# Seven sums of weights for the odd column tiles are formed in chunk 0 and not in chunk 1

## The chip, the cores and the metric

The kernel runs on one core of a Trainium2 chip, in fp32. The metric is the device time of one execution in microseconds; the time of a kernel is the median of its runs.

## What is computed

The reference runs a gated linear recurrence per batch and head, and a SwiGLU block on its output:

```
q, k, v, f_logit: (4, 8, 768, 48)
f = sigmoid(f_logit)
for t in range(768):
    state = f[t, :, None] * state + outer(k[t], v[t])
    y[t] = q[t] @ state
x = y as (4*768, 8*48) = (3072, 384)
out = (silu(x @ w_gate) * (x @ w_val)) @ w_out        # w_gate, w_val: (384, 1536), w_out: (1536, 384)
```

The weights come as float64 and are turned into fp32 on the chip.

## The kernel before

The 768 positions are cut into six chunks of 128. A chunk holds the 128 positions of all four batches, 512 tokens. Attention of a chunk is run batch by batch in steps (`attention`): gates through a sigmoid on ScalarE and, from chunk 2 on, a transpose on VectorE (L510, L511; the loads arrive in tiles called squares); a scan of the gates (L519), small steps (L522 to L524), kT (L531, L537), a second scan (L539) and qT (L532, L540) on VectorE; scores `sc` and transposed keys `kt` on TensorE (L552, L559), the masked scores `A` on VectorE (L554); the outputs `y` and the state's increment `dS` on TensorE (L578, L582, L606), and the state on VectorE (L610, L544). The steps of chunk c+1 are dealt out among the pieces of the feed-forward block of chunk c by `take_turns`, evenly by the number of pieces.

Chunk 0's feed-forward block is plain (`mlp_plain`). For 12 column tiles of 128 it runs gate and val products (L666), a silu on ScalarE (L678) and a product on VectorE (L682); then the down products (L690), which end in copies to `ob` (L695). Between these pieces stand calls of `weights`, each of which fetches a piece of weights by a transfer from SyncE's queue, splits an earlier one on ScalarE (L447, L449) and joins a still earlier one on VectorE in four instructions (L455 to L459). The joined gate and val weights stand together in `w_both`.

Chunks 1 to 5 use a scheme with 15 products for a 3 x 3 by 3 x 2 block product (`mlp_fifteen`) and one with seven for the down products (`down_seven`). The 15 products are run for each of four column tiles j, in the order 0, 2, 1, 3; the text calls the 15 products of one j a triple, as they come in three pieces. They need sums of blocks of the weights. Six of the results go to a tile of their own, `extra` (e0 to e5), formed by seven sums; nine sums are written into `w_both` itself, so they can only be formed after the plain products of chunk 0. Each sum is one VectorE instruction over 128 x 512 elements (`plus` L728, `minus` L731). `weight_sums(odd)` returns the 16 sums for the even (0) or the odd (1) column tiles. The even ones are needed from the first triple of chunk 1 on, the odd ones from the third.

In a triple the products of one name add up in one PSUM bank: A has two banks, B one, and the names o and c share two. After most products ScalarE copies the running sum out, to `c11` and so on or to `aside` (L841), and VectorE adds or subtracts it (L728, L731). Finished parts go through silu (L852) and a product on VectorE (L853) into `h`. A product into a bank waits for the copy of what stood there. The sigmoid and the silu need different tables on ScalarE, so a table load stands at each change between them.

What sets the order: the framework emits each engine's instructions into an in-order queue. A scheduler may move an instruction past others when it builds the queues; `keep_order` ties chosen instructions of an engine together. `chained` does so for the products and the copies of the triples. `behind(f)` ties what f emits to the last VectorE instruction emitted before it. `weave(first, second)` deals out the functions of `second`, two at a time, as pieces of their own among those of `first`, each pair through `behind`.

The lists of pieces are put together at the end of `short_path`, in the loop over the chunks. In chunk 0, `hidden` holds 24 gate and val pieces and 12 calls of `weights`, a call after every second piece, and `last` the 16 steps of the down products with four more calls. Before the change the 16 even sums are woven into `last`, and the 16 odd ones into the first half of chunk 1's pieces, so that

```
pieces = hidden + weave(last, weight_sums(0))
hidden = hidden[:1] + weave(hidden[1:half], weight_sums(1)) + hidden[half:]
```

Of the kernel before, what the change touches and what calls it, by code (L numbers as in the profile page):

```python
# [289 lines left out]
def short_path(ctx, tc, ident, least, judge, q, k, v, f_logit, moe_w_gate, moe_w_val, moe_w_out, out):  # L290
# [105 lines left out]
    def make_rooms(pool):  # L396
        for nm in "fkq":
            rooms[nm] = pool.tile([128, Q + HP * RUN], FP32, tag=f"{nm}squares", name=f"{nm}squares")
            nc.gpsimd.memset(rooms[nm][:, HP * RUN:], 0.0)
# [11 lines left out]
    def load(u):  # L411
        b, c = units[u]
        rows = slice(c * C, (c + 1) * C)
        for nm, src in (("f", f_logit), ("k", k), ("q", q)):
            if c >= SQUARES:
                for n in range(4):
                    at = Q * (1 - n % 2)
                    nc.sync.dma_start(
                        out=rooms[nm][Q * n:Q * (n + 1), at:at + HP * RUN].rearrange("t (a e) -> t a e", a=HP),
                        in_=src[b, n // 2::2, rows, :].rearrange("a (t i) d -> t a (i d)", i=NI))  # L420
                continue
            nc.sync.dma_start(out=raw[nm][u % NRAW][:, :, 0:D], in_=src[b, :, rows, :].rearrange("h t d -> t h d"))
        nc.sync.dma_start(out=v_of(u)[:, :, 0:D], in_=v[b, :, rows, :].rearrange("h t d -> t h d"))
# [205 lines left out]
    def attention_steps(c):  # L629

        runs = [attention(c * B + b) for b in range(B)]
        parts = [1, 2, 1, 2]
        order = sorted((2 * b + s, b, n) for b in range(B) for s, n in enumerate(parts))
        return [lambda b=b, n=n: [next(runs[b]) for _ in range(n)] for _, b, n in order]
# [11 lines left out]
    def keep_order(mine):  # L646
        for a, b in zip(mine, mine[1:]):
            tc.add_manual_dep(b, a.name, mybir.DependencyInfo(mybir.DependencyClass.NoSync,
                                                              mybir.DependencyReason.DATA), reason="order")
# [10 lines left out]
    def mlp_plain(c):  # L660
        h = {}

        def product(w, j, name):
            p = fps.tile([128, 512], FP32, tag="m", name=name)[:, 0:TB]
            for i in range(KT):
                nc.tensor.matmul(p, lhsT=w[:, i, j * 128:(j + 1) * 128], rhs=xT[c][:, i, :],  # L666
                                 start=(i == 0), stop=(i == KT - 1))
            return p

        def part(j):  # L670
            if j % NP not in h:
                h[j % NP] = hidden_tile()
            k = 2 * (j // NP)
            return h[j % NP][:, k:k + 2, :].rearrange("p a t -> p (a t)")

        def gate(j):
            p = product(w_gate, j, "gate")
            nc.scalar.activation(part(j), p, AF.Silu)  # L678

        def val(j):  # L680
            p = product(w_val, j, "val")
            nc.vector.tensor_tensor(part(j), part(j), p, ALU.mult)  # L682

        return ([lambda j=j, f=f: f(j) for i in range(0, NF, 2) for f in (gate, val) for j in (i, i + 1)],
                downs_abreast(c, h))
# [52 lines left out]
    def every_second(t, odd):  # L738

        return t.rearrange("p g (n two r) -> p g n two r", two=2, r=128)[:, :, :, odd, :]  # L740

    def weight_parts():
        w = {(i, k): w_both[:, :, k, i * NG:(i + 1) * NG] for i in range(KT) for k in range(KT)}
        e = [extra[:, n] for n in range(6)]
        return w, e

    def weight_sums(odd):

        w, e = weight_parts()
        w = {n: every_second(t, odd) for n, t in w.items()}  # L750
        e = [every_second(t, odd) for t in e]
        a11, a12, a13, a21, a22, a23, a31, a32, a33 = (w[i, k] for i in range(3) for k in range(3))
        return [lambda f=f, d=d, x=x, y=y: f(d, x, y) for f, d, x, y in (
            (minus, e[0], a11, a12), (plus, e[1], a12, a33), (plus, e[1], e[1], a13), (minus, e[2], e[1], a11),
            (minus, e[3], e[0], a13), (plus, e[4], a21, a32), (minus, e[5], a12, a21),
            (minus, a11, a12, a23), (plus, a13, e[3], a21), (plus, e[3], e[3], a23), (plus, a13, a13, a31),
            (minus, a13, a13, a33), (minus, a21, a22, a21), (plus, a22, a22, a23), (plus, a22, a22, a32),
            (minus, a31, a32, a31))]
# [237 lines left out]
    def weave(first, second):  # L996

        second = [second[i:i + 2] for i in range(0, len(second), 2)]
        woven = []
        for i, f in enumerate(first):  # L1000
            woven += [f] + [lambda fs=fs: behind(lambda: [g() for g in fs]) for fs in
                            second[i * len(second) // len(first):(i + 1) * len(second) // len(first)]]
        return woven

    def behind(f):

        n = len(traced)
        last = next(ins for ins in reversed(traced) if ins.engine == mybir.EngineType.DVE)
        f()
        keep_order([last] + [ins for ins in traced[n:] if ins.engine == mybir.EngineType.DVE])  # L1010

    def take_turns(first, second, rest):

        done = 0
        n = len(first) - rest
        for i, f in enumerate(first):
            f()
            want = min(i + 1, n) * len(second) // n
            for g in second[done:want]:
                g()  # L1020
            done = want
# [54 lines left out]
    for c in range(NCH):  # L1076
        if c == 0:
            hidden, last = mlp_plain(c)

            hidden = [f for i in range(NF) for f in hidden[2 * i:2 * i + 2] + [weights]]  # L1080
            for i in range(len(joins) - NF):
                last.insert(3 * i, weights)
            pieces = hidden + weave(last, weight_sums(0))
        else:
            hidden, last = mlp_fifteen(c)
            if c == 1:
                half = len(hidden) // 2
                hidden = hidden[:1] + weave(hidden[1:half], weight_sums(1)) + hidden[half:]
                hidden.append(lambda: behind(down_weight_sums))
            pieces = hidden + last  # L1090
        take_turns(pieces, attention_steps(c + 1) if c + 1 < NCH else [], 2 if c else 8)
        if c == 0:
            early.close()
            comb = ctx.enter_context(tc.tile_pool(name="comb", bufs=1))
            banks_a, banks_b, banks_o, later = (
                ctx.enter_context(tc.tile_pool(name=f"{n}ps", bufs=k, space=bass.MemoryType.PSUM))
                for n, k in (("A", 2), ("B", 1), ("o", 2), ("b", 3)))
            banks.append(later)
            make_rooms(comb)
            load(SQUARES * B)  # L1100
        if c == NCH - 2:
            judge(bank)
# [4 lines left out]
def kernel(  # L1107
# [22 lines left out]
    def judge(bank):  # L1130
# [9 lines left out]
                                   skip_runtime_bounds_check_because="a comparison"))  # L1140

    short_path(tc, ident, least, judge, *args)
    with tc.If(redo[0] > 0):
        general_path(tc, *args)
# [32 lines left out]
```

## Time and profile before

| | us |
|---|---|
| median of 5 runs | 634.19 |
| the five runs | 631.49, 632.08, 634.19, 634.79, 634.86 |
| the profiled execution | 633.19 |
| its span, first to last instruction | 631.4 |

| stage of the profiled execution | from, to (us) | length | VectorE busy |
|---|---|---|---|
| chunk 0, gate and val products | 36.5, 108.9 | 72.4 | 62.2 |
| chunk 0, down products | 110.5, 149.0 | 38.5 | 29.7 |
| chunk 1 | 149.0, 256.9 | 107.9 | 102.4 |
| chunk 2 | 256.9, 355.0 | 98.1 | 82.1 |
| chunk 3 | 355.0, 452.5 | 97.5 | 81.0 |
| chunk 4 | 452.5, 546.1 | 93.6 | 69.5 |
| chunk 5 | 546.1, 626.3 | 80.2 | 44.0 |

A stage is named after the feed-forward block that runs in it; the attention of the next chunk runs beside it. In the profile PE is TensorE's matmuls, PEld its weight loads, DVE is VectorE, ACT ScalarE, SP SyncE. A busy PE is not PE at its peak, since the matmuls are pipelined and their ends are modelled. A row of the timeline has its start, its length, engine, line, operation, output and input, the count, and in brackets the idle time of the engine ahead of it with what ended it. The durations of neighbours on VectorE and ScalarE overlap a little, so the text often takes the time from one start to the next.

### The profile page before, as it was taken

The numbers are of one execution on the slowest core, as the hardware profiler recorded it, in microseconds if no ns is written. First come the engines' busy times: TensorE is split into PE (matmuls) and PEld (weight loads), VectorE is DVE, ScalarE is ACT, GpSimd is POOL, SyncE is SP. The second block draws the span as 40 slices with busy tenths as digits, with TensorE's granted clock in tenths as the row PEclk, the third lists the DMA queues.
The fourth block names the chain that finished last, engine by engine and source line by source line (L and its number), as shares of the span: only waits on it lengthen the run. The fifth ranks groups of instructions, "written<-read, shape, count | busy, mean of one in ns | idle before, by whom it ended". The sixth has DMA issues, their size and how long they took to land.

```text
span 631.4 us, 10566 instructions
## 1 busy us (share of the span) xinstructions
PE 615.3 (97%) x3894; PEld 498.8 (79%) x3894; DVE 499.9 (79%) x941; ACT 288.2 (46%) x528; POOL 2.9 (0%) x22
## 2 busy tenths in 40 slices
PE   7999999999998999999999999999999999999996
PEld 4954545666777789888889988889988889988896
DVE  6888879968999999579997579998669992557641
ACT  1474655403764731466641365562175540166600
POOL 1000000000000000000000000000000000000000
PEclk8999999999998999999999999999999999999999
DMA  9997474106133122422323302323312200100001
GB/s 178 216 217 237 137 192 139 46 16 176 45 86 97 51 51 60 129 58 66 78 71 84 113 25 70 83 59 90 113 42 51 68 20 8 61 0 1 0 1 55
DMA packets 98395, 51.89 MB, mean 82 GB/s; under 512 B 56864, under 2 KB 92192, under 8 KB 98336
## 3 DMA queue, kind: packets, MB, share of 16 engines
q1 hardware_dynamic: 95024, 46.63, 30.8%
q10 hardware_dynamic: 3312, 4.52, 2.0%
q8 instruction: 32, 0.52, 0.4%
q14 instruction: 27, 0.22, 0.1%
HBM read 42.47 MB, written 4.72 MB: 75 GB/s over the span
## 4 chain that ended last, share of the span: by engine, by line
PE 82%; DVE 9%; SPq 3%; ACT 2%; issue 2%; DMA 2%; DVEq 0%; ACTq 0%
PE o L934 17%; PE A L836 14%; PE B L836 12%; PE gate L666 5%; PE val L666 5%; PE o L836 4%; PE c L836 4%; PE sc L552 4%; PE o L988 3%; PE y L582 3%; PE o L690 3%; PE y L578 2%; SPq L593 2%; PE kt L559 2%; DVE c L731 1%
## 5 line engine op out<-in xcount | busy, mean ns | idle before, releaser
L934 PE MATMUL o<-w_out,h 128*128 128x192 f32 x360 | 62.6, 330 | 0.7 <-DVE h L853 0.4
L836 PE MATMUL A<-xs,w_both 128*128 128x256 f32 x240 | 62.2, 381 | 0.1
L841 ACT COPY c<-A 128x512 f32<-128x512 f32 x40 | 23.4, 586 | 84.0 <-PE A L836 72.7
L934 PEld LDWEIGHTS o<-w_out,h 128*128 128x128 f32 x360 | 58.1, 190 | 2.6 <-ACT c L951 1.1
L728 DVE TENSOR_TENSOR c<-c,aside 128x512 f32<-128x512 f32 x60 | 41.6, 694 | 18.1 <-ACT aside L841 17.5
L841 ACT COPY aside<-A 128x512 f32<-128x512 f32 x60 | 35.0, 584 | 37.2 <-PE A L836 37.2
L836 PEld LDWEIGHTS A<-xs,w_both 128*128 128x128 f32 x240 | 44.9, 190 | 6.7 <-ACT aside L841 0.4
L853 DVE TENSOR_TENSOR h<-h,c 128x256 f32<-128x256 f32 x100 | 41.9, 430 | 8.2 <-ACT h L852 8.2
L731 DVE TENSOR_TENSOR c<-c,aside 128x512 f32<-128x512 f32 x60 | 41.8, 697 | 2.1 <-ACT aside L841 1.8
L836 PE MATMUL B<-xT,extra 128*128 128x256 f32 x160 | 41.8, 384 | 1.1 <-ACT aside L841 1.0
L852 ACT ACTIVATE h<-c 128x256 f32<-128x256 f32 x100 | 41.8, 420 | 2.1 <-DVE c L728 1.5
L836 PE MATMUL B<-xs,w_both 128*128 128x256 f32 x160 | 41.8, 384 | 0.0
L836 PE MATMUL c<-xT,w_both 128*128 128x256 f32 x160 | 41.7, 384 | 0.0
L836 PE MATMUL A<-xs,extra 128*128 128x256 f32 x160 | 41.1, 379 | 0.0
L934 PE MATMUL o<-ws,h 128*128 128x192 f32 x240 | 41.0, 327 | 0.0
L841 ACT COPY aside<-B 128x512 f32<-128x512 f32 x60 | 35.0, 584 | 10.7 <-PE B L836 10.5
L731 DVE TENSOR_TENSOR c<-o,c 128x512 f32<-128x512 f32 x40 | 27.6, 690 | 14.8 <-PE o L836 13.3
L934 PEld LDWEIGHTS o<-ws,h 128*128 128x128 f32 x240 | 39.1, 190 | 0.2
L552 PEld LDWEIGHTS sc<-qT,kT 48*128 48x128 f32 x384 | 25.1, 190 | 12.6 <-issue 6.4
L554 DVE TENSOR_TENSOR A<-sc,causal 128x512 f32<-128x512 f32 x48 | 31.0, 683 | 5.1 <-PE sc L552 5.1
L836 PEld LDWEIGHTS B<-xT,extra 128*128 128x128 f32 x160 | 29.8, 190 | 6.3 <-ACT aside L841 2.2
L586 ACT COPY yT<-y 128x256 f32<-128x256 f32 x40 | 14.4, 372 | 44.4 <-PE y L582 37.4
(132 smaller groups left out, 1195.5 us busy)
## 6 DMA issues: line engine op xcount, KB each, us to landing
fsquares<-in_f_logit_dram SPq DMA_DIRECT2D x64, 96.0 KB, 2.3
ksquares<-in_k_dram SPq DMA_DIRECT2D x64, 96.0 KB, 2.3
qsquares<-in_q_dram SPq DMA_DIRECT2D x64, 96.0 KB, 2.4
v<-in_v_dram SPq DMA_DIRECT2D x24, 192.0 KB, 3.6
w<-in_moe_w_gate_dram SPq DMA_DIRECT2D x6, 768.0 KB, 4.7
w<-in_moe_w_val_dram SPq DMA_DIRECT2D x6, 768.0 KB, 5.1
w<-in_moe_w_out_dram SPq DMA_DIRECT2D x6, 768.0 KB, 5.1
out_dram<-ob ACTq DMA_DIRECT2D x23, 192.0 KB, 2.4
```

Of the source, the lines that this page charges most:

```text
L552: nc.tensor.matmul(sc[par][:, a * C:(a + 1) * C], lhsT=kT[r, a, :], rhs=qT[r, a, :], start=True, stop=True)
L554: nc.vector.tensor_tensor(A[:, par], sc[par].rearrange("p (a t) -> p a t", t=C), causal.unsqueeze(1).broadcast_to((128, HP, C)), ALU.mult)
L582: nc.tensor.matmul(place(a, par), lhsT=v_[:, 2 * a + par, :], rhs=A[:, par, a, :], start=False, stop=a >= HP - 2, skip_group_check=True)
L666: nc.tensor.matmul(p, lhsT=w[:, i, j * 128:(j + 1) * 128], rhs=xT[c][:, i, :], start=(i == 0), stop=(i == KT - 1))
L690: nc.tensor.matmul(p, lhsT=h[n // 2][:, n % 2 * 2 + b // 2, b % 2 * C:(b % 2 + 1) * C], rhs=w_out[:, j, :], start=(n == 0), stop=(n == NF ...
L728: nc.vector.tensor_tensor(dst, a, b, ALU.add)
L731: nc.vector.tensor_tensor(dst, a, b, ALU.subtract)
L836: nc.tensor.matmul(p[name][:, n, :], lhsT=weights_of[a][:, n, cols], rhs=tokens[b], start=fresh and n == 0, stop=True, skip_group_check=True)
L841: nc.scalar.copy(t, p[name])
L852: nc.scalar.activation(dst, src[:, 0, :], AF.Silu)
L853: nc.vector.tensor_tensor(dst, dst, src[:, 1, :], ALU.mult)
L934: nc.tensor.matmul(p[:, n, :], lhsT=lhsTs[j][:, n * C:(n + 1) * C], rhs=rhs[:, j, :], start=first and j == 0 and n == 0, stop=j == NP - 1, ...
```

## The change

The list of `weight_sums` is put in another order: e0, e3 and e5 come first, then the four sums of e1, e2 and e4, then the nine that write into `w_both`. Sums 0, 1 and 2 of the even and of the odd list go, as three pieces of two, among the gate and val pieces of chunk 0, behind the 7th, the 8th and the 10th call of `weights`, tied with `behind`. The even and the odd sums 3 to 6 and the nine in-place even sums are woven into `last`. Only the nine in-place odd sums remain in chunk 1. With the three pieces and one more pair, chunk 0 has 64 pieces where it had 60, and chunk 1 has 25 where it had 28, so `take_turns` deals out the attention steps by other counts. What each sum computes is unchanged.

```diff
@@ weight_sums
         return [lambda f=f, d=d, x=x, y=y: f(d, x, y) for f, d, x, y in (
-            (minus, e[0], a11, a12), (plus, e[1], a12, a33), (plus, e[1], e[1], a13), (minus, e[2], e[1], a11),
-            (minus, e[3], e[0], a13), (plus, e[4], a21, a32), (minus, e[5], a12, a21),
+            (minus, e[0], a11, a12), (minus, e[3], e[0], a13), (minus, e[5], a12, a21),
+            (plus, e[1], a12, a33), (plus, e[1], e[1], a13), (minus, e[2], e[1], a11), (plus, e[4], a21, a32),
             (minus, a11, a12, a23), (plus, a13, e[3], a21), (plus, e[3], e[3], a23), (plus, a13, a13, a31),
             (minus, a13, a13, a33), (minus, a21, a22, a21), (plus, a22, a22, a23), (plus, a22, a22, a32),
             (minus, a31, a32, a31))]
@@ the loop over the chunks
             for i in range(len(joins) - NF):
                 last.insert(3 * i, weights)
-            pieces = hidden + weave(last, weight_sums(0))
+            sums_of = [weight_sums(odd) for odd in range(2)]
+            for n, at in enumerate((6, 7, 9)):
+                at = (at + 1) * 3 + n
+                hidden.insert(at, lambda n=n: behind(lambda: [t[n]() for t in sums_of]))
+            pieces = hidden + weave(last, sums_of[0][3:7] + sums_of[1][3:7] + sums_of[0][7:])
         else:
             hidden, last = mlp_fifteen(c)
             if c == 1:
                 half = len(hidden) // 2
-                hidden = hidden[:1] + weave(hidden[1:half], weight_sums(1)) + hidden[half:]
+                hidden = hidden[:1] + weave(hidden[1:half], sums_of[1][7:]) + hidden[half:]
                 hidden.append(lambda: behind(down_weight_sums))
             pieces = hidden + last
```

## The prediction

> **What bounds the kernel now.** I read the page first, then the busy time by stage, then TensorE's waits, then the two queues around the longest wait. All line numbers are those of the kernel before.
>
> ```profile
> PE 615.3 (97%) x3894; PEld 498.8 (79%) x3894; DVE 499.9 (79%) x941; ACT 288.2 (46%) x528; POOL 2.9 (0%) x22
> ```
>
> TensorE is busy nearly throughout; all it can still give is about 16 us. The stages say where. The columns are the stretch, its length, then busy time of PE, PEld, DVE, ACT, POOL, the granted clock, the DMA share and GB/s. The rows are the gate and val products of chunk 0, its down products, and chunks 1 and 2.
>
> ```profile
> 36.50:108.90 72.40, 72.40 (x306) 35.68 (x304) 62.24 (x98) 41.91 (x56) 0.00 (x0) 1.00 0.68 182
> 110.50:149.00 38.50, 38.50 (x227) 24.27 (x225) 29.69 (x54) 9.22 (x15) 0.24 (x3) 1.00 0.20 52
> 149.00:256.90 107.90, 102.39 (x686) 87.64 (x685) 102.36 (x193) 55.03 (x100) 0.00 (x0) 0.98 0.31 83
> 256.90:355.00 98.10, 97.98 (x682) 85.44 (x682) 82.08 (x159) 48.61 (x93) 0.00 (x0) 1.00 0.31 82
> ```
>
> Chunks 1 and 2 do the same products, yet chunk 1 takes 9.8 us more, and it alone has VectorE busy 102.4 of 107.9. That is the stage the change relieves; in chunk 0 TensorE never stops. The waits of TensorE (total, times, longest) and its timeline in chunk 1:
>
> ```profile
> PE sc L552 <- DVE qT L540: 2.4, 2, 1.8
> ...
> PE B L836 <- ACT aside L841: 1.0, 2, 0.5
> ```
> ```profile
> 177.82 1.16 PE L552 MATMUL sc<-qT,kT 48*128 48x128 f32 x16
> ...
> 183.21 1.13 PE L836 MATMUL B<-xT,extra 128*128 128x256 f32 x4 [0.48 <-ACT aside L841]
> ...
> 199.09 1.72 PE L552 MATMUL sc<-qT,kT 48*128 48x128 f32 x16 [1.79 <-DVE qT L540]
> ```
>
> The second batch's scores start at 177.82, just as their qT is ready; the third batch's wait 1.79 us for theirs. After that wait the granted clock, third from the right, falls:
>
> ```profile
> 197.00:199.10 2.10, 0.31 (x3) 0.01 (x1) 2.10 (x4) 1.24 (x4) 0.00 (x0) 1.00 0.76 208
> 199.10:201.00 1.90, 1.90 (x17) 1.68 (x18) 1.90 (x6) 0.00 (x0) 0.00 (x0) 0.61 0.77 190
> 201.00:203.20 2.20, 2.20 (x9) 1.89 (x9) 2.20 (x6) 0.58 (x1) 0.00 (x0) 0.56 0.26 52
> 203.20:206.00 2.80, 2.80 (x14) 2.27 (x13) 2.39 (x5) 1.71 (x2) 0.00 (x0) 1.00 0.00 0
> ```
>
> The price is 1.90 x 0.39 + 2.20 x 0.44 = 1.7 us on top of the 1.79.
>
> **The change, part by part.** Seven of the sixteen odd sums leave chunk 1 for chunk 0. One sum starts 0.60 us after the one before it (107.76 to 108.36), so 7 x 0.60 = 4.2 us of VectorE move; their number, 32, stays. No transfer or product is added.
>
> Chunk 0 gets six sums among gate and val, and one more among the down products. I walked VectorE's rows with them put in. The first pair stands behind qT at 79.11, the second behind the A products at 84.63; between there and 92.52 the queue stood idle 0.62, 1.11, 0.82 and 1.58 us, and the last two of these waits end on TensorE and ScalarE, so the 2.4 us vanish there. The third pair, 1.2 us, meets 0.30 us idle at 100.83 and one w_out join (0.87) that the new order puts behind the next qT: nothing left. That qT is the place to watch:
>
> ```profile
> 106.30 0.68 DVE L540 TENSOR_TENSOR qT<-qTp,head 128x512 f32<-128x512 f32 x1
> ```
> ```profile
> 108.91 1.16 PE L552 MATMUL sc<-qT,kT 48*128 48x128 f32 x16
> ```
>
> Ready at 106.98, used at 108.91: 1.9 us of cover. The fourth batch's qT moves from 126.40 to about 127.1 under a use at 129.66. The last join waited 2.69 us for TensorE at 129.77; two of the moved sums now fill that wait. Joins of the weights lie 3 to 6 us ahead of their products at this point (the last w_both join ends at 99.0, its val product starts at 103.67). The attention steps shift by one product at two places, as the diff spaces them over 56 pieces and not 52; the fetches on SyncE keep their order there but for two swaps of neighbours, and the sums themselves issue none. I take chunk 0 at nothing. If the cover were gone, it is 3.6 us at most; below nothing it can't go, as TensorE had no idle time there.
>
> In chunk 1 fewer sums also mean fewer pieces, so the attention steps fall on other products. The built order of the changed kernel puts the second batch's scores again behind the first 25 products, but the third batch's behind all 45 of three triples, where before they came after 41. And VectorE's order ahead of the second qT changes. I walk it with this trace's durations, TensorE arriving at 149.0 as before.
>
> ScalarE: aside copy at 159.18, table load 159.78 to 161.06, silu, aside copy, silu, aside copy to 162.90 (these two copies now come ahead of the sigmoid), table load to 164.2, sigmoid of the second batch done at 164.84; before it was done at 163.44.
>
> VectorE: gates transpose 164.88 (start to start 0.95), c11 0.60, two A products 1.20, two sums 1.20, so the scan L519 starts at 168.83; before at 169.04. Two sums taken out ahead were eaten by the later sigmoid and by A products that now stand behind it. From the scan to qT the old rows are
>
> ```profile
> 169.04 1.23 DVE L519 TENSOR_TENSOR_SCAN tails<-gates,ones 128x516 f32<-128x516 f32 x1
> ...
> 176.91 0.68 DVE L540 TENSOR_TENSOR qT<-qT,head 128x512 f32<-128x512 f32 x1
> ```
>
> which is 7.87 us. The new order has the same number of sums (two) in it, and besides a c12 subtraction, a c22 subtraction and two h products ahead of qT, which before came behind it: 2 x 0.60 + 2 x 0.335 = 1.87. The scan is followed by a sum of c22 and not by a transpose, which packs the small steps a little worse, 0.1. So qT starts at 168.83 + 7.87 + 1.97 = 178.7 and is ready at 179.4.
>
> TensorE comes sooner. First triple, 15 products at 0.865 = 12.97; the 1.24 of the ob wait at 151 stays; scores and kt 1.6; a wait of 0.45 for the aside copy (as 0.48 before); restarts 0.2: second triple at 165.4. Ten products 8.65, y and dS of the first batch 2.07, restarts 0.3: 176.45. Before this was 177.8. So TensorE now waits 179.45 - 176.45 = 3.0 us at the second batch, where it waited nothing. What queues behind is all of PE: the scores, the next product B, and with them every aside copy.
>
> At the third batch the scores have four products more ahead of them, 3.5 us, and VectorE's chain to its qT, started by c22 at about 190.3, ends near 199 for a use near 203: the 1.79 goes, and nothing is late there. The 0.48 at 183.21 goes too, as the table loads now end inside the new wait.
>
> The clock is the unknown. A gap of 1.08 us at 151 left it at 1.00; the gap of 1.79 us cost 1.7. The new gap of 3.0 us lies beyond both, nearest the second: 1.7, with 0 and 3.4 (twice as long) as ends. The old 1.7 goes with its wait, so the two cancel.
>
> [...]
>
> Sum to the common point (third batch done): second batch's scores later, 179.47 - 177.82 = +1.65; third batch's wait -1.79; aside wait -0.48; clock +1.70 - 1.70 = 0; chunk 0 at 0. Net -0.6 us. What follows, the down products with waits of 0.59, 0.36 and 0.30, has the same instructions with one 1.27 us ws sum now ahead of the last qT and 0.6 of c11 and a 0.53 idle time less: 0. Chunk 2 is reordered slightly under a cover of 8 us (qT at 283.49, used at 291.99). Against the profiled execution's 633.19 (span 631.4 and 1.8 around it) this is 632.6; the median of the runs shown, 634.19, lies 1.0 above that execution, and I forecast the median: 633.6.
>
> **Rivals.** First, faster: the second qT is in time, because ScalarE's or VectorE's short instructions pack better than I walked them. Then chunk 1 loses 1.79, 1.70, 0.48 and the 1.37 by which TensorE arrives sooner, 5.3 us; but VectorE still has 102.4 - 4.2 = 98.2 us to do and idles 5.5, so chunk 1 can't be under 103.7, and the gain is 4.2: 630.0. For it: the 7.87 us chain held no idle time, so any slack shows. Against it: the chain is longer by four instructions that the order fixes.
>
> Second, slower: the six early sums reach TensorE in chunk 0. VectorE is busy 30.99 of the 31.60 us from 94.7 to 126.3, so what does not vanish before 92.5 is carried on. It decides once the qT at 106.30 is more than 1.9 us late; its full price is 3.6 plus a clock loss of 1.7, with the -0.6 it is +4.7: 638.9. Against it: 4.1 us of idle time between 80 and 93.
>
> Third, nothing moves, because the wait only changes place. That is nearly my forecast, and falls in its range.
>
> **How the numbers follow.** My forecast, the wait moved from the third to the second batch, has 0.68, its own range 631.9 to 635.4 (clock ends of 1.7 either way); in time 0.19; chunk 0 late 0.13. Half a per cent, about what a measurement of this kernel can tell from no change, is 3.2 us: 631.0 and 637.4. So faster 0.19, same 0.68, slower 0.13. The range takes in the faster rival and the worse half of the clock's cost, and leaves out the slower one: 629.8 to 636.4.
>
> **What would show it.** Right: TensorE waits about 3 us for qT ahead of the second batch's scores in chunk 1, near 176 to 180, with a granted clock near 0.6 behind it; no wait at the third batch; chunk 0's end within 0.5 us of 149.0; chunk 1 about 107 us long. Wrong: no wait over 1 us there and a chunk 1 near 104, or gaps in TensorE between 80 and 149.

## The result, and the profile after the change

| | before | after |
|---|---|---|
| median, us | 633.59 (49 runs, 631.32 to 635.33) | 636.35 (28 runs, 632.34 to 640.44) |
| profiled execution, us | 633.19 | 637.1 |
| its span, us | 631.4 | 635.3 |

The ratio of the runs is 1.0041, with a 95% interval of 1.0028 to 1.0054. The change costs 2.8 us. That is less than half a per cent, so it falls in the forecast's middle case, and 636.35 is still inside the range, by 0.05 us: its upper end, 636.4, had been put there for the worse half of the clock's cost. But the forecast had the sign wrong: 0.6 us less, where the runs show more.

The stages first, with the same columns as before: chunk 0's gate and val products, its down products, chunks 1 and 2.

```profile
36.50:109.20 72.70, 72.70 (x309) 36.03 (x307) 64.32 (x103) 41.49 (x56) 0.00 (x0) 1.00 0.65 184
110.80:149.30 38.50, 38.50 (x227) 24.29 (x225) 30.96 (x55) 8.76 (x15) 0.24 (x3) 1.00 0.18 46
149.30:259.80 110.50, 104.26 (x686) 90.19 (x685) 100.16 (x186) 55.77 (x100) 0.00 (x0) 0.95 0.31 83
259.80:357.90 98.10, 97.68 (x676) 84.56 (x676) 83.00 (x159) 49.20 (x93) 0.00 (x0) 1.00 0.29 77
```

The reader is to see three things. TensorE is busy through all of chunk 0, as before. Chunk 1 grew from 107.9 to 110.5 us although VectorE does less in it (100.2 against 102.4). And its mean granted clock fell from 0.98 to 0.95. Of the signs that were named, a chunk 1 of about 107 us did not come. TensorE's waits, and then its timeline at the second, third and fourth batch of chunk 1:

```profile
PE sc L552 <- DVE qT L540: 4.5, 2, 2.8
...
PE o L837 <- ACT ob L695: 1.7, 1, 1.7
```
```profile
180.45 1.19 PE L552 MATMUL sc<-qT,kT 48*128 48x128 f32 x6 [2.82 <-DVE qT L540]
...
205.75 1.16 PE L552 MATMUL sc<-qT,kT 48*128 48x128 f32 x16
...
227.07 0.49 PE L552 MATMUL sc<-qT,kT 48*128 48x128 f32 x4 [1.72 <-DVE qT L540]
```

The wait did move from the third to the second batch, with 2.82 us where the forecast had 3.0. The fourth batch, which waited 0.59 us, now waits 1.72; before, its row was

```profile
225.05 1.16 PE L552 MATMUL sc<-qT,kT 48*128 48x128 f32 x16 [0.59 <-DVE qT L540]
```

Behind both waits the granted clock (third from the right) is low:

```profile
180.40:182.00 1.60, 1.55 (x7) 1.36 (x8) 1.60 (x3) 1.02 (x3) 0.00 (x0) 0.51 0.54 138
182.00:184.00 2.00, 2.00 (x8) 1.17 (x9) 2.00 (x4) 0.32 (x1) 0.00 (x0) 0.50 0.76 206
184.00:186.00 2.00, 2.00 (x12) 1.69 (x11) 1.29 (x3) 0.58 (x2) 0.00 (x0) 0.50 0.91 200
186.00:187.50 1.50, 1.50 (x5) 1.20 (x5) 1.50 (x5) 0.00 (x0) 0.00 (x0) 0.58 0.50 98
...
227.00:229.00 2.00, 1.93 (x11) 1.84 (x12) 2.00 (x4) 0.00 (x0) 0.00 (x0) 0.80 0.13 31
229.00:231.00 2.00, 2.00 (x9) 1.56 (x7) 2.00 (x3) 0.00 (x0) 0.00 (x0) 0.50 0.13 33
231.00:233.00 2.00, 2.00 (x14) 1.88 (x14) 2.00 (x6) 0.48 (x1) 0.00 (x0) 0.84 0.61 158
```

A clock of 0.50 is half speed: four matmuls of 128x256, which took 1.03 us at 176.60, took 2.07 at 181.57. In slices of 0.2 us the column reads 0.50 from 180.6 to 187.2, 0.56 and 0.87 in the slices at the two ends, and 1.00 before and after; so the share below 1.00, taken twice, is time at half speed. Behind the second batch that is 1.57 + 2.0 + 2.0 + 1.26 = 6.8 us, behind the old wait of the third batch it was 1.48 + 1.94 = 3.4 us. So the slow stretch is twice as long as the one it replaces, and behind the fourth batch stands a new one of 0.8 + 2.0 + 0.64 = 3.4 us.

The other executions agree. All those on record, grouped by their mean granted clock:

| mean clock | before, 95 executions (three sets of runs) | after, 30 executions |
|---|---|---|
| 0.996 and above | 45, median 632.8 us | 5, median 632.8 us |
| 0.993 to 0.995 | 45, median 634.0 us | 7, median 634.9 us |
| 0.992 and below | 5, median 635.5 us | 18, median 636.9 us |

In the executions with the highest mean clock the two kernels take the same time, though only five of the changed kernel are among them. The change moves executions into the last row.

### The profile page after: what moved, and what is told of

Read it like the earlier page. It is cut to its first block, busy times and chain, and to the rows that moved or that the text cites. A ratio compares the mean times of both kernels' runs of the same rounds, so it can differ in the third digit from the quotient of the medians.

```text
span 635.3 us, 10572 instructions
## 1 busy us (share of the span) xinstructions
PE 618.6 (97%) x3894; PEld 501.4 (79%) x3894; DVE 502.0 (79%) x941; ACT 289.5 (46%) x528; POOL 2.9 (0%) x22
## 4 chain that ended last, share of the span: by engine, by line
PE 87%; DVE 5%; issue 2%; ACT 2%; DMA 2%; SPq 1%; DVEq 0%; ACTq 0%
PE o L935 17%; PE A L837 15%; PE B L837 13%; PE o L837 5%; PE gate L666 5%; PE val L666 5%; PE c L837 5%; PE o L690 5%; PE sc L552 5%; PE o L989 3%; PE y L582 3%; PE y L578 2%; PE kt L559 2%; PE dS L606 1%; PE y L599 1%
## 5 line engine op out<-in xcount | busy, mean ns | idle before, releaser
L935 PE MATMUL o<-w_out,h 128*128 128x192 f32 x360 | 63.9, 335 | 0.0
L552 PEld LDWEIGHTS sc<-qT,kT 48*128 48x128 f32 x384 | 26.9, 194 | 16.2 <-issue 11.3
L552 PE MATMUL sc<-qT,kT 48*128 48x128 f32 x384 | 33.6, 297 | 4.5 <-DVE qT L540 4.5
L837 PEld LDWEIGHTS c<-xT,w_both 128*128 128x128 f32 x160 | 30.7, 193 | 4.8 <-ACT c L842 0.5
```

Source lines behind the costliest of these rows:

```text
L552: nc.tensor.matmul(sc[par][:, a * C:(a + 1) * C], lhsT=kT[r, a, :], rhs=qT[r, a, :], start=True, stop=True)
L837: nc.tensor.matmul(p[name][:, n, :], lhsT=weights_of[a][:, n, cols], rhs=tokens[b], start=fresh and n == 0, stop=True, skip_group_check=True)
L935: nc.tensor.matmul(p[:, n, :], lhsT=lhsTs[j][:, n * C:(n + 1) * C], rhs=rhs[:, j, :], start=first and j == 0 and n == 0, stop=j == NP - 1, ...
```

## The experiments

The theory at the start: the cost lies in the qT that now come late to TensorE in chunk 1, and in the slow clock behind them, and the waits come from where `take_turns` now puts the attention steps (25 pieces where there were 28). The rivals: the early sums cost in chunk 0; or only the amount of VectorE's work counts.

Where a text says "every queue in its own order", all instructions of a kernel were tied with `keep_order` to the order that its queues had, so that nothing moves but what is named; `marks` holds instructions noted where they are emitted. The ratios are to the kernel before, with 95% intervals.

**The ws sum behind the fourth qT** (`e1_ws_after_q`).

```diff
+        if engine == "DVE":
+            mine.remove(marks["ws"])
+            mine.insert(mine.index(marks["q", 2, 3]) + 1, marks["ws"])
```

> The changed kernel with every queue in its own order, except that VectorE forms the ws sum (1.27 us) right behind the fourth batch's qT of chunk 1 and not right ahead of it. Theory (the change costs through qT that come late to TensorE, and through the slow clock behind those waits): the wait at the fourth batch's scores falls from 1.72 to about 0.45 us, the slow clock behind it (about 1.7 us) goes too, together 3.0 us: a profiled execution near 634.1 where the changed kernel had 637.1, a median near 633.4. Rival (the sum only changes place and is late for the down products that use ws): as the changed kernel, 636 to 637.

Measured: 636.58 us, ratio 1.0035 (1.0012 to 1.0058), not told apart from the changed kernel. TensorE's timeline:

```profile
227.01 0.49 PE L554 MATMUL sc<-qT,kT 48*128 48x128 f32 x4 [0.45 <-DVE qT L541]
228.50 2.22 PE L939 MATMUL o<-w_out,h 128*128 128x192 f32 x12 [1.01 <-DVE h L858]
```

The wait for qT is 0.45 us as expected, but the sum now stands ahead of an h product, and TensorE waits 1.01 us for that: 1.46 in all for 1.72. The rival is right on the wait. The clock did stay at 1.00 at this place: from the fourth batch's scores to the last product group of the down products it is 29.24 us without the new wait, 1.5 less than in the changed kernel. But behind the second batch the clock was at half speed for 10.2 us here and not 6.8, which took most of that back (26.59 us to the third batch's scores where the changed kernel had 25.30). One of its rows:

```profile
188.00:190.00 2.00, 2.00 (x6) 1.55 (x6) 0.45 (x1) 0.59 (x1) 0.00 (x0) 0.50 0.00 0
```

**The sums moved, the steps at their old places** (`e2_old_spacing`).

```diff
-                hidden = hidden[:1] + weave(hidden[1:half], sums_of[1][7:]) + hidden[half:]
+                hidden = hidden[:1] + weave(hidden[1:half], [lambda: None] * 7 + sums_of[1][7:]) + hidden[half:]
```

> The changed kernel with seven empty functions in chunk 1 in the places of the sums that left it, so that the attention steps fall between the same products as before the change; the seven sums stay in chunk 0. Theory (the waits come from where the steps now fall; the move of the sums by itself is a gain): no wait over 1 us at the second and at the fourth batch, the third batch's wait of 1.79 us shorter or gone, chunk 1 about 104 us long, median 630 to 631, ratio to the kernel before about 0.995. Rival (the early sums cost in chunk 0 as much as they save): ratio 1.000 or more.

Measured: 634.10 us, ratio 1.0007 (0.9991 to 1.0022). The second batch is in time again (its scores run at 178.88 without a wait), so the place of the steps made that wait. But there is no gain, against the theory's second half, and the ratio is the one that the rival had: the third batch waits as long as it ever did, and a join of w_out in chunk 0 is now late. In this trace the part of chunk 0 behind the third scores is 0.84 us longer than before, and chunk 1 up to its last product group 0.55 shorter.

```profile
127.94 2.85 PE L690 MATMUL o<-w_out,h 128*128 128x384 f32 x8 [0.57 <-DVE w_out L459]
...
199.10 1.16 PE L552 MATMUL sc<-qT,kT 48*128 48x128 f32 x16 [1.72 <-DVE qT L540]
```

VectorE's queue says why chunk 1 gained so little. Between the gates transpose that starts the third batch's chain (183.93 before, 183.98 here) and its qT (198.29 and 198.33) it holds the same four sums, all of them in-place ones, which the change leaves in chunk 1. The seven sums that left stood before the second qT, where TensorE had not waited.

**The steps moved, the sums at their old places** (`e3_sums_stay`), the kernel before with the sixteen sums as five pieces:

```diff
-                hidden = hidden[:1] + weave(hidden[1:half], weight_sums(1)) + hidden[half:]
+                hidden = hidden[:1] + weave(hidden[1:half], in_five(weight_sums(1))) + hidden[half:]
```

> The kernel before, all sixteen odd sums in chunk 1 and none moved, but handed out as five pieces (4, 3, 3, 3, 3) instead of eight, so that the attention steps of chunk 1 fall where they fall after the change. Theory (the place of the steps makes the waits): TensorE waits at the second batch for 2.8 to 5.2 us (up to four more sums of 0.60 stand ahead of that qT than in the changed kernel) and at the fourth for about 1.7, each with a slow clock behind it; median 638 to 641, slower than the changed kernel. Rival one (the sums in chunk 0 are what costs): faster than the changed kernel, near 633.6. Rival two (only the number of sums on VectorE counts, not the place of the steps): as the kernel before, waits at the third batch.

Measured: 638.00 us, ratio 1.0078 (1.0051 to 1.0105), slower than the changed kernel: all six runs took 637.2 us or more, where that has a median of 636.35. TensorE waits at all three batches: 2.21 us at the second (and 0.87 for a copy before it), 1.24 at the third, 2.32 at the fourth. The second wait is shorter than expected, the third was not expected. The clock fell behind the second and the fourth, for 3.4 us each.

```profile
181.54 0.94 PE L552 MATMUL sc<-qT,kT 48*128 48x128 f32 x12 [2.21 <-DVE qT L540]
```

With the second experiment this separates the two parts of the change. New places alone: +4.0 us on 634.02. Sums alone: +0.1. Both: +2.8, as the sums that left make the new places a little less bad: with them gone the three waits are 2.82, 0 and 1.72 us. Both rivals of this experiment fall.

**TensorE kept busy in the second wait** (`e4_warm`).

```diff
+        n_warm = {(2, 1): 9}.get((c, b), 0)
+        some = ones.bitcast(mybir.dt.bfloat16)
+        for _ in range(n_warm):
+            nc.tensor.matmul(sc[0], lhsT=some[:, 0:128], rhs=some[:, 0:512], start=True, stop=True)
```

> The changed kernel with every queue in its own order, and nine short bf16 matmuls on a constant put into TensorE's queue ahead of the second batch's scores in chunk 1, into the bank that the scores then overwrite: they run while TensorE waits there for qT. Theory (the slow clock follows from the idle gap, and costs about 3.4 us there): qT and the scores come at the same time as in the changed kernel, near 180.4, the granted clock behind them is 1.00 and not 0.50, and the execution is 3.4 us shorter: near 633.7 by profile, 633.0 median. Rival (the clock falls for another reason, or the slow clock hides behind other work): clock near 0.5 again, or a time as the changed kernel's, 636 to 637.

Measured: 634.91 us, ratio 1.0014 (0.9999 to 1.0030). The timeline, and the clock behind:

```profile
176.94 2.10 PE L553 MATMUL sc<-ones 128*128 128x512 bf16 x9
179.84 0.71 PE L560 MATMUL sc<-qT,kT 48*128 48x128 f32 x6 [0.79 <-DVE qT L540]
```
```profile
179.84:182.00 2.16, 2.16 (x18) 1.66 (x19) 2.16 (x4) 1.42 (x4) 0.00 (x0) 1.00 0.61 151
```

From the second batch's scores to the third's it is 201.97 - 179.84 = 22.13 us, where the changed kernel took 205.75 - 180.45 = 25.30: the slow clock cost 3.17 us there. The median falls by 1.4 where 3.4 was expected. By the table above not every execution loses as much as the profiled one; that this accounts for the whole difference isn't shown.

**The early sums twice** (`e5_early_twice`).

```diff
-                hidden.insert(at, lambda n=n: behind(lambda: [t[n]() for t in sums_of]))
+                hidden.insert(at, lambda n=n: behind(lambda: [t[n]() for t in sums_of * 2]))
```

> The changed kernel with the six early sums among chunk 0's gate and val products formed twice (the second time with the same result): 3.6 us more for VectorE there. Theory (that stretch has room; 1.7 of the 4.1 us of idle time between 80 and 93 are left, and the qT used at 109 has 1.9 us of cover): no wait at those scores or one under 0.5 us; the joins of w_out come up to 1.9 us later, so waits of 0.5 to 1.5 us in all at chunk 0's down products; chunk 0 ends 0.5 to 1.5 us later than in the changed kernel, median 636.5 to 638. Rival (early sums reach TensorE in full): 3.6 us and a slow clock, 640 or more.

Measured: 639.21 us, ratio 1.0070 (1.0045 to 1.0095), above what the theory gave. Yet its trace shows the theory's picture in chunk 0: no wait at any scores, 0.42 us at a join of w_out. From the third scores of chunk 0 to the first product of chunk 1 it is 152.53 - 111.76 = 40.77 us, 0.7 more than in the changed kernel. The profiled execution had lost 2.5 us before 60 us, where the kernels are alike (last section). So the trace does not bear out this median as the price of the sums; `e11_q3_early_twice`, below, puts the same question on a kernel whose runs lie closer together.

**The second qT ahead** (`e6_q_ahead`).

```diff
+            mine.remove(marks["q", 2, 1])
+            mine.insert(mine.index(marks["turned", 2, 1]) + 1, marks["q", 2, 1])
```

> The changed kernel with every queue in its own order, except that VectorE forms the second batch's qT of chunk 1 right behind the transpose of its raw part, ahead of eight other instructions (2.8 us and more of them) that stood before it. Theory: no wait over 0.3 us at the second batch's scores and no slow clock behind them; TensorE comes up to 6 us sooner to the fourth batch and waits 2 to 3.5 us there, with a slow clock; profiled execution 631 to 633 where the changed kernel had 637.1, median 632 to 633.5. Rival (the wait comes back at once, as the eight delayed instructions hold PSUM banks that the next products need): waits of over 1.5 us in the second and third triple, median 635 to 637.

Measured: 633.92 us, ratio 1.0018 (0.9996 to 1.0040). The second batch's scores start without a wait at 177.95; small waits of 0.23, 0.18, 0.54 and 0.63 us come back in the triples; the fourth batch waits 2.31 us and loses the clock (0.60 from 227 to 229). That is the theory's picture in the waits, but not its times: the median is 0.4 us above the range, and the profiled execution took 634.78 us where 631 to 633 was expected.

**The third qT ahead, in the kernel before and with the sums moved** (`e7_before_q3`, `e8_spaced_q3`). The same edit in both:

```diff
+            mine.remove(marks["head", 2, 2])
+            mine.insert(mine.index(marks["kT", 2, 2]) + 1, marks["head", 2, 2])
+            mine.remove(marks["q", 2, 2])
+            mine.insert(mine.index(marks["head", 2, 2]) + 1, marks["q", 2, 2])
```

> The kernel before, no sum moved, every queue in its own order, except that VectorE forms head and qT of the third batch of chunk 1 right behind that batch's kT, ahead of six instructions of the triple that stood before them. Theory (what costs is the place of one qT in VectorE's queue, not the amount of VectorE's work in chunk 1): the wait of 1.79 us at the third batch goes, and the slow clock behind it, without a sum being moved; up to 1 us comes back in the triple; median 630.8 to 632.2, ratio to the kernel before 0.995 to 0.998. Rival (VectorE's load is the bound): the wait comes back in the triple or at the fourth batch, ratio 1.000.

> The kernel with the seven sums in chunk 0 and the attention steps where they fell before the change (e2_old_spacing), and the same move of head and qT of the third batch right behind its kT as in e7_before_q3. Theory: the third batch's wait of 1.72 us goes with its slow clock; median 630.8 to 632.2. If moving the sums is worth something once no qT is late, it is faster than e7_before_q3 by up to 1 us, else equal to it. Rival (VectorE's load is the bound): faster than e7_before_q3 by 1.8 us or more, as 4.2 us of sums are out of chunk 1.

Measured: 633.26 us, ratio 0.9995 (0.9982 to 1.0009), for the first; 632.08 us, ratio 0.9974 (0.9962 to 0.9985), for the second, which is thereby faster than both kernels of this case. In both the third batch's wait is gone. In both TensorE then comes earlier to the fourth batch and waits twice as long there, with the same gap and a different fate of the clock; the first kernel's wait and a row behind it, then the second's:

```profile
226.83 1.16 PE L556 MATMUL sc<-qT,kT 48*128 48x128 f32 x16 [1.26 <-DVE qT L543]
```
```profile
229.00:231.00 2.00, 2.00 (x8) 2.00 (x7) 2.00 (x3) 0.00 (x0) 0.00 (x0) 0.50 0.11 25
```
```profile
223.01 1.16 PE L556 MATMUL sc<-qT,kT 48*128 48x128 f32 x16 [1.25 <-DVE qT L543]
```
```profile
224.00:226.00 2.00, 1.65 (x12) 1.35 (x9) 2.00 (x5) 0.00 (x0) 0.00 (x0) 1.00 0.12 29
```

Moving one qT alone gave nothing that its interval shows, and moving the sums alone gave nothing; both together gave 0.26%. By the two medians, whose intervals just overlap, the sums are worth 1.2 us once the third qT no longer comes late; the theory had up to 1, the rival 1.8 and more.

**Both waits kept busy, after and before** (`e9_warm_both`, `e10_before_warm`). The edit of `e4_warm`, with nine matmuls ahead of the second and six ahead of the fourth batch's scores in the changed kernel, and six ahead of the third's in the kernel before.

> The changed kernel with every queue in its own order, and short bf16 matmuls on a constant in TensorE's queue at both of its late qT in chunk 1: nine ahead of the second batch's scores, six ahead of the fourth's. The waits stay, the idle gaps shrink to 0.8 us and 0.5 us or less. Theory (of the 2.7 us that the change costs, the waits themselves are about 0.5 and the slow clock behind them the rest): granted clock 1.00 behind both, median 633.0 to 633.7; against e10_before_warm, where the same is done for the kernel before, 0.3 to 1.2 us more. Rival (the waits or the early sums are the cost, the clock is not): 634.9 as e4_warm or more, and 2 us or more above e10_before_warm.

> The kernel before with every queue in its own order, and six short bf16 matmuls on a constant in TensorE's queue ahead of the third batch's scores in chunk 1, where it waits 1.79 us for qT. Theory: the wait stays, the clock behind it is 1.00, 1.0 to 1.7 us less than the kernel before in the median (a few executions keep the clock without help): 632.2 to 632.9. Rival: as the kernel before, 633.6 to 634.

Measured: 633.29 us, ratio 0.9998 (0.9982 to 1.0014), for the changed kernel; 633.79 us, ratio 1.0010 (0.9993 to 1.0027), for the kernel before. The clock is 1.00 behind every one of these waits. TensorE at the second and the fourth batch of the changed kernel, and the clock behind the second:

```profile
181.63 0.71 PE L560 MATMUL sc<-qT,kT 48*128 48x128 f32 x6 [0.83 <-DVE qT L540]
...
225.31 0.49 PE L560 MATMUL sc<-qT,kT 48*128 48x128 f32 x4 [0.64 <-DVE qT L540]
```
```profile
181.63:184.00 2.37, 2.37 (x20) 1.87 (x20) 2.37 (x5) 1.58 (x5) 0.00 (x0) 1.00 0.64 158
```

The first lands as expected: the scores still wait for their qT (they start 30.79 us behind chunk 1's first product, 31.10 in the changed kernel), but the clock is kept, and the 2.8 us of the change are gone. The second is a miss. Its trace shows the saving (from the third scores to the fourth, without the fourth's own wait, 23.75 us for 25.37). But that execution, 635.50 us and so 1.7 above the median, also shows three places that took it back: everything is 1.34 us later at the third scores of chunk 0, the wait for ob at chunk 1's start is 1.73 and not 1.08, and a wait of 1.33 us for ob stands in chunk 3 (452.50) that the kernel before did not show. Why the median did not fall stays open, and it can't price the old clock loss.

The difference of the two medians is -0.5 and not +0.3 to +1.2, and the traces say the same: from chunk 1's first product to its last product group it is 103.65 us in the changed kernel and 105.12 in the kernel before, both with the clock kept. Without the clock the change costs nothing that these runs show.

**The early sums twice, on the faster kernel** (`e11_q3_early_twice`): `e8_spaced_q3` with each of the six formed twice in its place.

```diff
-                hidden.insert(at, lambda n=n: behind(lambda: [t[n]() for t in sums_of]))
+                hidden.insert(at, lambda n=n: behind(lambda: [twice(t[n]) for t in sums_of]))
```

> e8_spaced_q3 with every queue in its own order, and each of the six early sums among chunk 0's gate and val products formed twice in its place (the second time with the same result): 3.6 us more for VectorE there. Theory (chunk 0 has room for them but for what reaches the joins of w_out): 0 to 1 us more than e8_spaced_q3, 632.1 to 633.1. Rival (chunk 0's VectorE has no room, as e5_early_twice's median of 639.2 would have it): 2.9 us or more, 635 and up.

Measured: 632.62 us, ratio 0.9984 (0.9970 to 0.9998), 0.5 us above `e8_spaced_q3`. 3.6 us of extra VectorE work among the gate and val products cost half a microsecond. So the sums alone do not explain the median of `e5_early_twice`.

**The fourth wait of the faster kernel kept busy** (`e12_q3_warm4`): four short matmuls ahead of the fourth batch's scores in `e8_spaced_q3`.

> e8_spaced_q3 with every queue in its own order, and four short bf16 matmuls on a constant ahead of the fourth batch's scores in chunk 1, where TensorE still waits 1.25 us for qT. Theory (a gap of that length loses the clock in some executions: one of 1.26 us did in e7_before_q3, this one of 1.25 us did not): equal to e8_spaced_q3 or up to 0.5 us less, 631.5 to 632.1. Rival (the gap is too short to matter): no difference.

Measured: 632.60 us, ratio 0.9978 (0.9964 to 0.9992). That is 0.5 us above the range, and by the intervals no difference to `e8_spaced_q3`, whose executions had mean clocks of 0.995 to 0.999 as they were. Filling this gap gained nothing that shows.

## Why the prediction was wrong

The sum of the prediction against the two profiled executions. The chain is cut at the first product of chunk 1 (149.00 and 149.35), the first product of the fourth triple (205.88 and 207.33), and the last product group of chunk 1's down products (254.83 and 257.83).

| step | predicted | measured |
|---|---|---|
| second batch's scores later | +1.65 | +2.28 |
| third batch's wait | -1.79 | -1.79 |
| wait for aside at 183.21 | -0.48 | -0.48 |
| clock, new less old | 0 | 3.17 - 1.62 = +1.55 |
| the rest up to the fourth triple | none | -0.46 |
| **to the fourth triple** | **-0.6** | **+1.10** |
| fourth batch and down products | 0 | +1.55 |
| **chunk 1** | **-0.6** | **+2.65** |

**Chunk 0 at nothing: nearly right.** The qT at 106.58 is ready 2.0 us before the scores at 109.27, and the profiled execution lost nothing:

```profile
106.58 0.68 DVE L540 TENSOR_TENSOR qT<-qTp,head 128x512 f32<-128x512 f32 x1
```

What the walk missed is the joins of w_out. From the third scores of chunk 0 to chunk 1's start it is 40.1 us in all four kernels without early sums and in three of the eight that form them once, but 40.6 to 40.9 in the other five (`e1`, `e2`, `e6`, `e9`, `e12`), each with a wait of 0.2 to 0.57 us for a join. The slower rival's mechanism is there, but at the joins and not at the scores, and at 0.9 us or less where the rival had 5.3.

Chunk 1 starts at 149.35, within the 0.5 us of 149.0 that was named as a sign of the forecast.

**The walk of chunk 1 to the second qT: right.** The second batch's scores were put 30.47 us behind the start of chunk 1 and came at 31.10. The 0.6 is the wait for ob, 1.70 where 1.08 was taken; it was 1.08 to 1.73 over the runs of this study. The third batch's wait is gone, as forecast.

**The clock, taken as 1.7 against 1.7: the step that failed.** The new gap of 2.82 us cost 3.17 and not 1.7. The prediction named 3.4 as an end and took the value of the nearest row, a gap of 1.79 us. But one row could not give the price: in these runs it came in units of 3.4 us at half speed, one of which the old row showed (last section), and behind gaps of 2.81 to 2.87 us three traces show one, two and three of them. And the old loss was not a sure one: 45 of 95 executions of the kernel before kept a mean clock of 0.996 or more, where the profiled one, with the loss, has 0.993.

**The fourth batch, put at 0: a wait and its clock loss not seen.** The text saw "one 1.27 us ws sum now ahead of the last qT" and set 1.13 us of gone work against it. In the queue the sum is the last thing ahead of qT; the first row is qT before the change, the other two are after it:

```profile
224.23 0.67 DVE L540 TENSOR_TENSOR qT<-qT,head 128x512 f32<-128x512 f32 x1
```
```profile
224.94 1.38 DVE L731 TENSOR_TENSOR ws<-w_out 128x1152 f32<-128x1152 f32 x1
226.20 0.73 DVE L540 TENSOR_TENSOR qT<-qT,head 128x512 f32<-128x512 f32 x1
```

So qT starts 1.97 us later: 1.26 for the sum, 0.27 for a state instruction that now also stands behind the raw transpose, and 0.43 because that transpose is later. TensorE comes only 0.89 us later, and the wait grew by 1.1. In return the three waits behind these scores, 0.36, 0.30 and 0.31 us, are gone. With the longer gap came a clock loss: 30.86 us from these scores to the cut in `e4_warm`, where the clock falls (0.54 from 224 to 226), against 29.18 in `e9_warm_both`, where it doesn't (1.00 from 225.3 on), 1.7. Without it the stretch comes to -0.1, so the 0 was right but for the clock.

**The rest of the sum: right.** Chunk 1 took 2.65 us more. Less the 1.55 of the table's clock row and the 1.7 of the fourth batch it is -0.6, as forecast. That it fits so closely is in part luck: the 0.6 more for ob and the -0.46 of the rest, which the sum did not have, nearly cancel. What failed is the clock in both places, and the wait at the fourth batch that brought the second loss.

**The stage that "the change relieves".** The faster rival counted 4.2 us of VectorE time as a possible gain of chunk 1. `e2_old_spacing` shows that this was the wrong measure: the sums that left stood in a stretch of the queue ahead of a qT for which TensorE had not waited.

The profiled executions differ by 3.9 us of span. 2.65 are chunk 1 and 0.36 the start; the last 0.9 lies behind the cut, where the profiles of this study vary from 376.5 to 378.6 us, so it isn't put down to the change.

Three things stay open: why the slow clock lasted two units in the changed kernel, three in `e1_ws_after_q` and one in `e5_early_twice` behind gaps of 2.82, 2.81 and 2.87 us; why `e5_early_twice` lost so much more in the median than in its chunk 0; and why the median of `e10_before_warm` did not fall.

## What to carry to other kernels

Look for the stretch of a busy engine's queue between the event that starts a chain and the consumer that waits for it: here seven sums moved out of another stretch gave nothing, one qT put ahead of other work gave nothing clear, and the two together gave 0.26%. When the order comes from counting pieces, a change in their number is a change of its own, and here the larger one: lay out where each step falls before and after, and price that first. Price a gap in front of TensorE not at its length alone but with a possible loss of the clock: here gaps from 1.07 us on lost it in some executions. Short matmuls that fill the gap are worth a try; they took 1.4 and 3.1 us off the changed kernel's median, and nothing in `e10_before_warm` and `e12_q3_warm4`.

## What the runs showed of the hardware

**The slow clock came in units of 3.4 us.** Time at half speed, from the clock column: behind the third batch before 3.4 us; behind the fourth batch after 3.4; in `e7_before_q3` at the fourth batch 0.12 + 2.0 + 1.32 = 3.4; in `e5_early_twice` at the second batch 3.4; behind the second batch after 6.8; in `e1_ws_after_q` there 10.2. That is once, twice and three times. At half speed it would cost 1.7, 3.4 or 5.1 us; the traces price one unit at 1.62 and 1.7 us and two at 3.17. The gaps that lost it here were 1.07 us (`e5_early_twice`, at the kernel's start) to 2.87 us long (the same run, second batch of chunk 1). What sets the unit of 3.4 us no run shows.

**Gaps of the same length kept the clock in one run and lost it in another.** A gap of 1.07 us at the kernel's start (TensorE waits for a transfer of fraw) lost it in `e5_early_twice` and kept it in `e6_q_ahead`; both rows are of the stretch behind it.

```profile
19.00:21.00 2.00, 2.00 (x24) 1.91 (x22) 0.00 (x0) 0.32 (x1) 0.00 (x0) 0.50 1.48 168
```
```profile
19.00:21.00 2.00, 2.00 (x26) 1.88 (x26) 1.00 (x2) 0.56 (x2) 0.00 (x0) 1.00 1.46 170
```

In the first the clock was at half speed for 6.8 us, and the third scores of chunk 0 came 2.5 us later than in the changed kernel's profile. Such a loss comes ahead of all that the change touches, and in an execution that has it, it is about as large as what the change costs. The 1.25 and 1.26 us gaps of `e8_spaced_q3` and `e7_before_q3` above are a second such pair.

**A granted clock of 1.00 in the rows was not full speed at the very start of two runs.** In `e9_warm_both` and `e10_before_warm` the twelve matmuls on a constant with which the kernel keeps TensorE busy at its start (`idle`, at 9.76) took 5.16 and 5.13 us with a clock of 1.00 in the rows, where `e6_q_ahead` took 2.75 for them.
